# Where q and k are loaded, cast and transposed in an attention and MLP kernel

## The chip, the cores and the metric

The kernel runs on one core of one Trainium2 chip. The metric is the device time of one execution in microseconds. Of nine executions of the kernel before, the median is 354.95 us (353.53 to 356.51). One further execution was recorded by the hardware profiler; every line of a profile in this document is from such an execution. TensorE multiplies matrices, VectorE and ScalarE do elementwise work, GpSimd (POOL) does elementwise work and issues DMA transfers, and SyncE (SP) only issues DMA transfers. In the profile they are PE (PEld for its weight loads), DVE, ACT, POOL and SP; a q after a name means the engine's instruction queue.

## The reference

Eight batches of eight heads, 576 positions, head dimension 64. For each head, with q, k, v in float32 and a vector s:

```python
scores = scale * np.matmul(q, k.transpose(0, 1, 3, 2))
cum = np.cumsum(np.maximum(s, 0.0), axis=-1)
bias = -(cum[:, :, :, None] - cum[:, :, None, :])
scores = np.where(causal, -1e9, scores + np.minimum(bias, 0.0))
attn = softmax(scores)                       # with 1e-9 added to the sum
x = np.matmul(attn, v)                       # -> 4608 tokens x 512
out = (gelu_exact(x @ w_in)) @ w_out         # 512 -> 2048 -> 512
```

The output is 4608 x 512 in float32. The kernel computes the decay as weights on the keys: `wb` holds exp(cum) for each key, v is multiplied by it into `vv`, and the same weights give the denominator.

## The kernel before, in words

The 4608 tokens are taken in nine chunks of 512 (the loop over `c`, L554). Chunk c does three things: layer 1 of its tokens (`l1_item`, 64 matmuls that fill `h_ps`, L472), layer 2 (`l2_item`, 64 matmuls that fill `o_ps`, L491, in four parts of 16 matmuls, each copied by VectorE to one of three `o_sb` buffers at L498 and written out by SP at L500), and, between the parts of layer 2, the attention of batch nb = c + 1. A batch is 576 tokens, so attention stays ahead of the MLP. Attention of a batch goes by pairs of heads (four pairs): scores (`sc_item`, L366, from `qkT`), exp on ScalarE (L372), the causal mask on VectorE (L381, L386), then `av_item` (L394: `avn` the numerator, `avd` the denominator, `avr` for the last 64 positions), and the normalised result goes to `xT`, which layer 1 reads.

The order on every engine is that of the program: the schedule is written by hand, and an engine that waits holds up all that is behind it in its own queue. Waits follow from the program's order: an instruction waits for those ahead of it in the text that write what it reads, or that use what it overwrites.

How q and k reach `qkT` (two of them, used in turn by even and odd batches):

- Batches 0 and 1: `load_early` has POOL issue DMA transfers that cast float32 to bfloat16 on the way, in runs of nine rows of one head (2304 bytes read, 1152 written). TensorE transposes them (`tr_item`, L349) and VectorE copies the result to `qkT` (L354).
- Batches 2 to 7: `load_qk` (L151) has SP issue one float32 load for q and one for k, in runs of six rows (1536 bytes), into one buffer each. POOL casts them in eight pieces (`cast`, L166) into `qk_bf`, with the two heads of a pair beside each other. SP writes `qk_bf` to DRAM (`write_rows`, L174) and reads it back with eight transposing DMA transfers (`transpose_rows`, L181), for four pairs, q and k each.

v of each batch is loaded by SP in five transfers (`load_v`, L192) into one of two buffers, scaled by VectorE (`scale_v`, L220) and reduced to its largest magnitude (`absmax_v`, L210). `absmax` (L203) reduces q and k of a pair from `qkT`. These maxima decide at the very end whether the fast path was safe to use.

In a chunk from 1 to 6 SP's row is: v of batch nb + 1, rows of nb + 1 for q and k, loads of q and k of nb + 2; then the output of part 0, the transposes of pair 0 of batch nb + 1, output 1, the transposes of pair 1, output 2, the transposes of pairs 2 and 3, output 3. VectorE's row is: `scale_v(nb)`, `absmax_v(nb)`, `absmax(c, p)` for the four pairs of batch c, and then the masks, normalisations and `o_sb` copies of the chunk.

Of the kernel before, what the change touches and what calls it, by code (L numbers as in the profile page):

```python
# [19 lines left out]
def kernel(  # L20
# [10 lines left out]
    nc = tc.nc  # L31
    fp32 = mybir.dt.float32
    bf16 = mybir.dt.bfloat16
# [5 lines left out]
    B, H, S, D = q.shape  # L39
    scale = 1.0 / (D ** 0.5)  # L40
    BH = B * H
    ST = 5
    NR = 6
    PR = S // NR
    SL = S - 512
    NP = H // 2
    dff = moe_w_in.shape[1]
    KO = (H * D) // 128
# [46 lines left out]
    G = 9  # L95
    early = {}

    def load_early(b, n, p, both=False):
        src = q if n == "q" else k
        if b == 0 and p == 0:  # L100
            early[n] = work.tile([128, 2, 2, 2, G * D], bf16, tag=f"raw{n}", bufs=1, name=f"early_{n}")
        e0 = (p // 2) * 64
        out = early[n][e0 : e0 + 64, b, p % 2]
        if both:
            out = early[n][e0 : e0 + 64, b].rearrange("g j e f -> g (j e) f")
        ap = [[G * D, 64], [S * D, 4 if both else 2], [1, G * D]]
        nc.gpsimd.dma_start(
            out=out,
            in_=bass.AP(tensor=src.tensor, offset=src.offset + (b * H + 2 * p) * S * D, ap=ap),
        )  # L110
# [21 lines left out]
    w_in_r = const.tile([128, KO, dff], bf16, name="w_in_r")  # L132
    w_out_r = const.tile([128, FT, KO * 128], bf16, name="w_out_r")
    vv = [const.tile([128, ST, H, D], bf16, name=f"vv{i}") for i in range(2)]
    qkT = [const.tile([128, 2, NP, 640], bf16, name=f"qkT{i}") for i in range(2)]
# [8 lines left out]

    def load_qk(b, n, p0, p1, eng):
        src = q if n == "q" else k
        if p0 == 0:
            raws[b, n] = work.tile([PR, H, NR, D], fp32, tag=f"raw{n}", bufs=1, name=f"raw_{n}")  # L150
        eng.dma_start(  # L151
            out=raws[b, n][:, 2 * p0 : 2 * p1].rearrange("p h r d -> p h (r d)"),
            in_=bass.AP(
                tensor=src.tensor,
                offset=src.offset + b * H * S * D + 2 * p0 * S * D,
                ap=[[NR * D, PR], [S * D, 2 * (p1 - p0)], [1, NR * D]],
            ),
        )

    qk_of = {}  # L160

    def cast(b, n, p, eng):
        i = 0 if n == "q" else 1
        if (b, i) not in qk_of:
            qk_of[b, i] = work.tile([PR, NP, NR, 2, D], bf16, tag="qkbf", bufs=2, name="qk_bf")
        eng.tensor_copy(  # L166
            qk_of[b, i][:, p].rearrange("p r e d -> p e r d"), raws[b, n][:, 2 * p : 2 * p + 2]
        )

    rows_of = {}  # L170

    def write_rows(b, i, eng):
        rows_of[b, i] = t = dram.tile([NP, S, 128], bf16, name=f"rows{b}_{i}")
        eng.dma_start(  # L174
            out=t.rearrange("j (p r) c -> p j (r c)", r=NR),
            in_=qk_of.pop((b, i)).rearrange("p j r e d -> p j (r e d)"),
        )

    def transpose_rows(b, p):
        for i in range(2):  # L180
            nc.sync.dma_start_transpose(out=qkT[b % 2][:, i, p, :S], in_=rows_of[b, i][p])  # L181

    def v_tile(b):
        raws[b, "v"] = work.tile([128, ST, H, D], fp32, tag="rawv", bufs=2, name="raw_v")

    def load_v(b, engs):
        if (b, "v") not in raws:
            v_tile(b)
        t = raws[b, "v"]
        for st in range(ST):  # L190
            n_st = 128 if st < ST - 1 else SL
            engs[st % len(engs)].dma_start(  # L192
                out=t[:n_st, st, :, :],
                in_=bass.AP(
                    tensor=v.tensor,
                    offset=v.offset + b * H * S * D + st * 128 * D,
                    ap=[[D, n_st], [S * D, H], [1, D]],
                ),
            )
# [143 lines left out]
    def tr_item(b, p, i):  # L343
        t_ps = ps.tile([128, G, 64], bf16, tag="av", bufs=3, name="tr_ps")
        e0 = (p // 2) * 64
        src = early["qk"[i]]
        for r in range(G):
            for e in range(2):
                nc.tensor.transpose(  # L349
                    t_ps[e * 64 : e * 64 + 64, r, :],  # L350
                    src[e0 : e0 + 64, b, p % 2, e, r * D : (r + 1) * D],
                    ident_bf[e0 : e0 + 64, e0 : e0 + 64],
                )
        nc.vector.tensor_copy(  # L354
            qkT[b % 2][:, i, p, :S].rearrange("d (g r) -> d g r", r=G), t_ps.rearrange("d r g -> d g r")
        )
# [186 lines left out]
    scale_pair(0, 3)  # L543
    for i in range(4):
        load_w(1, i)
    for p in (0, 2):
        for n in "qk":
            load_early(1, n, p, both=True)
    for p in range(NP):
        av_item(0, p, wide=p in (1, 2), rest=False)  # L550
    nc.gpsimd.memset(amv, 0.0)
    nc.gpsimd.memset(ones, 1.0)

    for c in range(NCH):  # L554
        nb = c + 1
        l1_item(c, 0, 0, KO - 1)
        l1_item(c, 1, 0, KO - 1)
        if c == 0:
            for p in range(NP):
                av_rest(0, p)  # L560
            norm_rest(0)
        l1_item(c, 0, KO - 1)
        l1_item(c, 1, KO - 1)
        l1_item(c, 2, av=True)
        if 0 < c and nb < B:
            if nb + 1 < B:
                load_v(nb + 1, [nc.sync])
                for i, n in enumerate("qk"):
                    for p in range(NP):
                        cast(nb + 1, n, p, nc.gpsimd)  # L570
                    write_rows(nb + 1, i, nc.sync)
            if nb + 2 < B:
                for n in "qk":
                    load_qk(nb + 2, n, 0, NP, nc.sync)
            scale_v(nb, STS, nc.vector)
            absmax_v(nb)
        if c == 0:
            absmax_v(0)
        if c < B:
            for p in range(NP):  # L580
                absmax(c, p)
        for f2 in range(3, FT // 2):
            l1_item(c, f2)
        if c == 0:
            exp_set()
            l2_item(c, 0, av=True)
            load_v(1, [nc.sync])
            for n in "qk":
                load_qk(2, n, 0, NP, nc.sync)
            tr_pair(1, 0)  # L590
            tr_pair(1, 1)
            l2_item(c, 1, 0, 4)
            tr_pair(1, 2)
            l2_item(c, 1, 4, 8)
            tr_pair(1, 3)
            sc_item(1, 0)
            l2_item(c, 1, 8)
            load_v(2, [nc.sync])
            for i, n in enumerate("qk"):
                for p in range(NP):  # L600
                    cast(2, n, p, nc.gpsimd)
            sc_item(1, 1)
            l2_item(c, 2, 0, 6, av=True)
            sc_item(1, 2)
            scale_pair(1, 0)
            l2_item(c, 2, 6, 12, av=True)
            sc_item(1, 3)
            scale_pair(1, 1)
            l2_item(c, 2, 12, av=True)
            l2_item(c, 3, 0, 4)  # L610
            for i in range(2):
                write_rows(2, i, nc.sync)
            av_item(1, 0)
            scale_pair(1, 2)
            scale_pair(1, 3)
            l2_item(c, 3, 4, 8)
            av_item(1, 1, wide=True)
            l2_item(c, 3, 8, 12)
            av_item(1, 2, wide=True)
            l2_item(c, 3, 12)  # L620
            av_item(1, 3)
            norm_rest(1)
            for p in range(NP):
                transpose_rows(2, p)
            for n in "qk":
                load_qk(3, n, 0, NP, nc.sync)
            absmax_v(1)
            cert_decay()
        elif nb < B:
            exp_set()  # L630
            l2_item(c, 0, 0, 4)
            sc_item(nb, 0)
            l2_item(c, 0, 4)
            for p in range(1, NP):
                if nb + 1 < B:
                    transpose_rows(nb + 1, p - 1)
                sc_item(nb, p)
                av_item(nb, p - 1)
                l2_item(c, p, 0, 12)
                if p == NP - 1:  # L640
                    if nb + 1 < B:
                        transpose_rows(nb + 1, p)
                    av_item(nb, p)
                    norm_rest(nb)
                l2_item(c, p, 12)
        else:
            if c == B - 1:
                cert_1()
            for sub in range(4):
                l2_item(c, sub, av=sub % 2 == 0)  # L650
                if c == B - 1 and sub < 3:
                    (cert_2, cert_3, cert_4)[sub]()
# [151 lines left out]
```

## Time and profile before

| | |
|---|---|
| median of nine executions | 354.95 us |
| the profiled execution | 354.31 us |
| its span, first to last instruction | 352.5 us |
| PE busy | 321.7 us (91%) |
| ACT busy | 202.1 us (57%) |
| DVE busy | 195.0 us (55%) |
| POOL busy | 60.7 us (17%) |
| DMA moved | 54.38 MB |
| DMA queue of SP (q1) | 86160 packets, 47.35 MB |
| DMA queue of POOL (q0) | 6464 packets, 6.55 MB |
| median time to landing of raw_q / raw_k / rows / a transpose | 12.7 / 14.7 / 5.6 / 3.4 us |

The page gives each engine's busy time, then the span in 40 slices of 8.8 us with the busy share in tenths, the clock that TensorE was granted, and the share of the 16 DMA engines; then the chain of work that ended last, followed back from the end; then groups of instructions by line. In a line of a timeline the first number is the start in microseconds from the span's start, the second the duration. A line of waits reads: who waited, for whom, microseconds in total, how many times, the longest. A landing time is counted from the start of the issue of a transfer to its last byte.

### The profile page before, as it was taken

Reading aid. Unit: us, or ns where it says so; the run is one execution under the profiler, and the core shown is the slowest. Engines: PE = TensorE matmul, PEld = TensorE weight load, DVE = VectorE, ACT = ScalarE, POOL = GpSimd, SP = SyncE. Lnnn points to the kernel's source line nnn. Section 1 sums busy time; section 2 is a strip of 40 time slices with the busy share of each in tenths; the row PEclk is TensorE's granted clock in tenths of the full one; section 3 lists DMA queues with packets and bytes.
Section 4 is the critical chain, followed back from the end, with each engine's and each line's share of the span. In section 5 each row is a group of like instructions: output and inputs, shape, how many; then the busy total and the mean of one; then the engine's idle time right before and its main releaser. Section 6 shows DMA issues by size and latency. Waiting matters only on the chain.

```text
span 352.5 us, 6310 instructions
## 1 busy us (share of the span) xinstructions
PE 321.7 (91%) x2538; PEld 164.7 (47%) x2538; DVE 195.0 (55%) x363; ACT 202.1 (57%) x286; POOL 60.7 (17%) x85
## 2 busy tenths in 40 slices
PE   1778999899999557999999999999999999999993
PEld 1553454544554224544554455445544554444441
DVE  4596576799650295478357745764485548050011
ACT  2676628587666441675777676767576757403500
POOL 6590000700240700340070015000000000000000
PEclk9999999999999986999999999999999999999999
DMA  7999969994999989999999999772430100011011
GB/s 150 157 206 198 191 143 215 227 244 104 236 235 257 210 179 284 234 169 234 267 178 185 270 231 201 150 184 65 130 63 0 56 37 31 0 62 60 0 62 66
DMA packets 92660, 54.38 MB, mean 154 GB/s; under 512 B 67984, under 2 KB 87952, under 8 KB 92624
## 3 DMA queue, kind: packets, MB, share of 16 engines
q1 hardware_dynamic: 86160, 47.35, 60.9%
q0 software_dynamic: 6464, 6.55, 11.2%
q8 instruction: 22, 0.36, 0.4%
q14 instruction: 14, 0.11, 0.1%
HBM read 36.85 MB, written 16.52 MB: 151 GB/s over the span
## 4 chain that ended last, share of the span: by engine, by line
PE 70%; DVE 13%; SPq 5%; DMA 5%; ACT 3%; issue 2%; POOL 0%; DVEq 0%; ACTq 0%; POOLq 0%
PE o_ps L491 31%; PE h_ps L472 27%; PE sc_ps L366 4%; SPq L192 4%; DMA out_dram<-o_sb 4%; DVE vv L220 3%; PE avn L394 3%; DVE amx L203 3%; PE avd L394 2%; DVE amv L210 2%; DMA early_k<-in_k_dram 2%; DVE qkT L354 2%; ACT P L372 1%; SPq L151 1%; PE tr_ps L349 1%
## 5 line engine op out<-in xcount | busy, mean ns | idle before, releaser
L491 PE MATMUL o_ps<-w_out_r,gT 128*128 128x512 bf16 x576 | 136.5, 387 | 4.0 <-DVE o_sb L498 4.0
L472 PE MATMUL h_ps<-xT,w_in_r 128*128 128x512 bf16 x576 | 126.3, 379 | 2.0 <-DVE xT L427 1.4
L372 ACT ACTIVATE P<-sc_ps 128x1024 bf16<-128x1024 f32 x64 | 62.0, 1021 | 49.8 <-PE sc_ps L366 49.8
L472 PEld LDWEIGHTS <-w_in_r 128*128 128x128 bf16 x576 | 56.1, 98 | 69.9 <-issue 2.7
L491 PEld LDWEIGHTS <-gT 128*128 128x128 bf16 x576 | 53.9, 99 | 67.4 <-issue 9.3
L478 ACT ACTIVATE gT<-h_ps 128x1024 bf16<-128x1024 f32 x54 | 54.3, 1022 | 47.2 <-PE h_ps L472 47.1
L498 DVE COPY o_sb<-o_ps 128x512 f32<-128x512 f32 x36 | 24.7, 687 | 74.5 <-PE o_ps L491 58.9
L381 DVE TENSOR_TENSOR P<-P,tri_bf 128x512 bf16<-128x512 bf16 x61 | 27.3, 451 | 40.8 <-ACT P L372 40.2
L166 POOL CAST qk_bf<-raw_q 96x768 bf16<-96x768 f32 x24 | 20.5, 890 | 142.9 <-DMA raw_q<-in_q_dram 142.9
L203 DVE TENSOR_REDUCE amx<-qkT 128x2 f32<-128x1152 bf16 x32 | 40.9, 1335 | 0.0
L427 DVE SCALAR_TENSOR_TENSOR xT<-avn,ln 128x256 bf16<-128x256 f32 (+3 forms) x64 | 21.6, 384 | 23.6 <-ACT ln L412 23.6
L220 DVE TENSOR_TENSOR vv<-raw_v,wb 128x512 bf16<-128x512 f32 (+2 forms) x46 | 29.5, 700 | 0.0
L411 ACT ACTIVATE ln<-avd 128x256 f32<-128x256 f32 x56 | 18.6, 391 | 18.6 <-PE avd L394 18.6
L366 PE MATMUL sc_ps<-qkT 64*128 64x256 bf16 (+2 forms) x320 | 22.4, 266 | 3.7 <-DVE qkT L354 3.6
L394 PEld LDWEIGHTS <-vv 128*64 128x64 bf16 x384 | 18.0, 114 | 15.7 <-issue 12.1
L412 ACT ACTIVATE ln<-ln 128x512 f32<-128x512 f32 (+1 forms) x40 | 23.5, 587 | 1.3
L481 ACT ACTIVATE gT<-h_ps 128x512 bf16<-128x512 f32 x36 | 19.6, 603 | 6.3 <-PE h_ps L472 6.3
L394 PE MATMUL avn<-P,vv 128*64 128x256 bf16 x224 | 16.8, 274 | 6.8 <-DVE P L381 6.1
L210 DVE TENSOR_REDUCE amv<-raw_v 128x1 f32<-128x2048 f32 (+1 forms) x16 | 22.9, 1470 | 0.0
L366 PEld LDWEIGHTS <-qkT 64*128 64x128 bf16 x320 | 13.9, 99 | 18.4 <-issue 11.7
L166 POOL CAST qk_bf<-raw_k 96x768 bf16<-96x768 f32 x24 | 20.3, 885 | 4.1 <-DMA raw_k<-in_k_dram 1.6
L394 PEld LDWEIGHTS <-wb 128*64 128x64 bf16 x384 | 18.2, 116 | 0.2
(79 smaller groups left out, 140.5 us busy)
## 6 DMA issues: line engine op xcount, KB each, us to landing
out_dram<-o_sb SPq DMA_DIRECT2D x36, 256.0 KB, 2.6
raw_v<-in_v_dram SPq DMA_DIRECT2D x32, 256.0 KB, 5.0
raw_q<-in_q_dram SPq DMA_DIRECT2D x6, 1152.0 KB, 12.7
raw_k<-in_k_dram SPq DMA_DIRECT2D x6, 1152.0 KB, 14.7
rows<-qk_bf SPq DMA_DIRECT2D x12, 576.0 KB, 5.6
w_in_r<-in_moe_w_in_dram POOLq DMA_DIRECT2D x4, 512.0 KB, 8.1
w_out_r<-in_moe_w_out_dram POOLq DMA_DIRECT2D x4, 512.0 KB, 13.1
raw_v<-in_v_dram SPq DMA_DIRECT2D x8, 128.0 KB, 4.5
```

What stands on the lines that cost most here:

```text
L166: eng.tensor_copy(qk_of[b, i][:, p].rearrange("p r e d -> p e r d"), raws[b, n][:, 2 * p : 2 * p + 2])
L203: nc.vector.tensor_reduce(amx[:, b * NP + p], qkT[b % 2][:, :, p, :S], axis=AX, op=ALU.max, apply_absolute_value=True)
L210: nc.vector.tensor_reduce(amv[:n_st, b, j : j + 1], t[:n_st, st0:st1].rearrange("p s h d -> p (s h d)"), axis=AX, op=ALU.max, apply_absolu ...
L220: eng.tensor_tensor(vb[:n_st, st0:st1, h0:h1, :], t[:n_st, st0:st1, h0:h1, :], wb[:n_st, st0:st1, b * H + h0 : b * H + h1] .unsqueeze(3).t ...
L366: nc.tensor.matmul(s_ps[:, e, off : off + n], lhsT=qkT[b % 2][e * 64 : e * 64 + 64, 1, p, jt * 128 : jt * 128 + 128], rhs=qkT[b % 2][e * 6 ...
L372: nc.scalar.activation(P[:, :, UO[u] : UO[u] + UW[u]], s_ps[:, :, : UW[u]], func=AF.Exp, scale=scale)
L381: eng.tensor_tensor(d, d, tri_bf.unsqueeze(1).unsqueeze(1).to_broadcast([128, 2, 2, 128]), op=MULT)
L394: nc.tensor.matmul(out[e * 64 : e * 64 + 64, lo : lo + n], lhsT=(wb[:, jt, b * H + h : b * H + h + 1].to_broadcast([128, 64]) if den else ...
L472: nc.tensor.matmul(h_of[c, f2][i], lhsT=w_in_r[:, ko, ft * 128 : (ft + 1) * 128], rhs=xT[:, ko, c * NB % XW : c * NB % XW + NB], start=(ko ...
L478: nc.scalar.activation(gT_of[c][:, f2 * 2 : f2 * 2 + 2, :], hh_of[c, f2], func=AF.Gelu)
L491: nc.tensor.matmul(o_ps, lhsT=gT[:, ft, sub * 128 : (sub + 1) * 128], rhs=w_out_r[:, ft, :], start=(ft == 0), stop=(ft == FT - 1),)
L498: nc.vector.tensor_copy(o_sb, o_ps)
```

## The change

`load_qk` is rewritten: for batches 1 to 7 it calls `load_early` four times (two pairs at a time, q and k), so that all q and k come by POOL's casting transfers in runs of 2304 bytes, into one of three buffers for q and one of three for k. POOL's eight casts become four copies (`interleave`) from bfloat16 to bfloat16 that set the two heads of a pair beside each other, and the rows are written in runs of 2304 bytes. v of batch 1 is issued earlier: POOL first writes a few elements of its buffer from the last columns of `w_in_r`, so that SP's loads wait until w_in is there. Batches 2 and 3 are loaded by POOL before the loop begins; in chunk c POOL copies batch nb + 1 and then issues the loads of nb + 2. In chunks 1 to 5 the eight transposes of batch nb + 1 are issued right behind its rows, at the head of the chunk, ahead of `absmax` and of the chunk's outputs; in chunk 0, pairs 0 and 1 of batch 2 stand before output 3 and pairs 2 and 3 behind it.

```diff
     def load_early(b, n, p, both=False):
-        if b == 0 and p == 0:
-            early[n] = work.tile([128, 2, 2, 2, G * D], bf16, tag=f"raw{n}", bufs=1, name=f"early_{n}")
+        if p == 0:
+            early[b, n] = work.tile([128, 2, 2, G * D], bf16, tag=f"raw{n}", bufs=3, name=f"early_{n}")
...
-    def load_qk(b, n, p0, p1, eng):
-            raws[b, n] = work.tile([PR, H, NR, D], fp32, tag=f"raw{n}", bufs=1, name=f"raw_{n}")
-        eng.dma_start(
...
-    def cast(b, n, p, eng):
-            qk_of[b, i] = work.tile([PR, NP, NR, 2, D], bf16, tag="qkbf", bufs=2, name="qk_bf")
-        eng.tensor_copy(
-            qk_of[b, i][:, p].rearrange("p r e d -> p e r d"), raws[b, n][:, 2 * p : 2 * p + 2]
-        )
...
+    def load_qk(b):
+        for p in (0, 2):
+            for n in "qk":
+                load_early(b, n, p, both=True)
+    def interleave(b, n):
+        t = qk_of[b, i] = work.tile([128, 2, G, 2, D], bf16, tag="qkbf", bufs=2, name="qk_bf")
+        for j in range(2):
+            nc.gpsimd.tensor_copy(
+                t[:, j].rearrange("g r e d -> g e r d"),
+                early[b, n][:, j].rearrange("g e (r d) -> g e r d", r=G),
+            )
...
+    load_qk(1)
+    v_tile(1)
+    nc.gpsimd.tensor_copy(
+        raws[1, "v"][:, :, 0, 0], w_in_r[:, KO - 1, dff - 1 : dff].to_broadcast([128, ST])
+    )
+    load_v(1, [nc.sync])
...
+    for b in (2, 3):
+        load_qk(b)
+    for n in "qk":
+        interleave(2, n)
...
                 load_v(nb + 1, [nc.sync])
                 for i, n in enumerate("qk"):
-                    for p in range(NP):
-                        cast(nb + 1, n, p, nc.gpsimd)
+                    interleave(nb + 1, n)
                     write_rows(nb + 1, i, nc.sync)
-            if nb + 2 < B:
-                for n in "qk":
-                    load_qk(nb + 2, n, 0, NP, nc.sync)
+                if nb + 2 < B:
+                    load_qk(nb + 2)
+                for p in range(NP):
+                    transpose_rows(nb + 1, p)
             scale_v(nb, STS, nc.vector)
             absmax_v(nb)
...
             for p in range(1, NP):
-                if nb + 1 < B:
-                    transpose_rows(nb + 1, p - 1)
                 sc_item(nb, p)
```

More of the change, by code (lines that the diff above doesn't have):

```diff
@@ L42 @@
     ST = 5
-    NR = 6
-    PR = S // NR
     SL = S - 512
@@ L99, in load_early @@
         src = q if n == "q" else k
-        if b == 0 and p == 0:
-            early[n] = work.tile([128, 2, 2, 2, G * D], bf16, tag=f"raw{n}", bufs=1, name=f"early_{n}")
+        if p == 0:
+            early[b, n] = work.tile([128, 2, 2, G * D], bf16, tag=f"raw{n}", bufs=3, name=f"early_{n}")
         e0 = (p // 2) * 64
-        out = early[n][e0 : e0 + 64, b, p % 2]
+        out = early[b, n][e0 : e0 + 64, p % 2]
         if both:
-            out = early[n][e0 : e0 + 64, b].rearrange("g j e f -> g (j e) f")
+            out = early[b, n][e0 : e0 + 64].rearrange("g j e f -> g (j e) f")
         ap = [[G * D, 64], [S * D, 4 if both else 2], [1, G * D]]
@@ L143 @@
     raws = {}
-    def load_qk(b, n, p0, p1, eng):
-        src = q if n == "q" else k
-        if p0 == 0:
-            raws[b, n] = work.tile([PR, H, NR, D], fp32, tag=f"raw{n}", bufs=1, name=f"raw_{n}")
[L151 to L157, printed above, removed]
-        )
+    def load_qk(b):
+        for p in (0, 2):
+            for n in "qk":
+                load_early(b, n, p, both=True)
     qk_of = {}
-    def cast(b, n, p, eng):
+    def interleave(b, n):
         i = 0 if n == "q" else 1
-        if (b, i) not in qk_of:
-            qk_of[b, i] = work.tile([PR, NP, NR, 2, D], bf16, tag="qkbf", bufs=2, name="qk_bf")
-        eng.tensor_copy(
-            qk_of[b, i][:, p].rearrange("p r e d -> p e r d"), raws[b, n][:, 2 * p : 2 * p + 2]
-        )
+        t = qk_of[b, i] = work.tile([128, 2, G, 2, D], bf16, tag="qkbf", bufs=2, name="qk_bf")
[4 more added lines that the diff above has]
+            )
     rows_of = {}
     def write_rows(b, i, eng):
-        rows_of[b, i] = t = dram.tile([NP, S, 128], bf16, name=f"rows{b}_{i}")
+        rows_of[b, i] = t = dram.tile([2, 2, S, 128], bf16, name=f"rows{b}_{i}")
         eng.dma_start(
-            out=t.rearrange("j (p r) c -> p j (r c)", r=NR),
+            out=t.rearrange("j a (g r) c -> (a g) j (r c)", r=G),
             in_=qk_of.pop((b, i)).rearrange("p j r e d -> p j (r e d)"),
@@ L180, in transpose_rows @@
         for i in range(2):
-            nc.sync.dma_start_transpose(out=qkT[b % 2][:, i, p, :S], in_=rows_of[b, i][p])
+            nc.sync.dma_start_transpose(out=qkT[b % 2][:, i, p, :S], in_=rows_of[b, i][p % 2, p // 2])
     def v_tile(b):
@@ L345, in tr_item @@
         e0 = (p // 2) * 64
-        src = early["qk"[i]]
+        src = early[b, "qk"[i]]
         for r in range(G):
@@ L350, in tr_item @@
                     t_ps[e * 64 : e * 64 + 64, r, :],
-                    src[e0 : e0 + 64, b, p % 2, e, r * D : (r + 1) * D],
+                    src[e0 : e0 + 64, p % 2, e, r * D : (r + 1) * D],
                     ident_bf[e0 : e0 + 64, e0 : e0 + 64],
@@ L545 @@
         load_w(1, i)
-    for p in (0, 2):
-        for n in "qk":
-            load_early(1, n, p, both=True)
+    load_qk(1)
[4 more added lines that the diff above has]
+    load_v(1, [nc.sync])
     for p in range(NP):
@@ L568 @@
                 for i, n in enumerate("qk"):
-                    for p in range(NP):
-                        cast(nb + 1, n, p, nc.gpsimd)
+                    interleave(nb + 1, n)
                     write_rows(nb + 1, i, nc.sync)
-            if nb + 2 < B:
-                for n in "qk":
-                    load_qk(nb + 2, n, 0, NP, nc.sync)
+                if nb + 2 < B:
+                    load_qk(nb + 2)
+                for p in range(NP):
+                    transpose_rows(nb + 1, p)
             scale_v(nb, STS, nc.vector)
@@ L586 @@
             l2_item(c, 0, av=True)
-            load_v(1, [nc.sync])
-            for n in "qk":
-                load_qk(2, n, 0, NP, nc.sync)
             tr_pair(1, 0)
@@ L598 @@
             load_v(2, [nc.sync])
-            for i, n in enumerate("qk"):
-                for p in range(NP):
-                    cast(2, n, p, nc.gpsimd)
+            for i in range(2):
+                write_rows(2, i, nc.sync)
             sc_item(1, 1)
@@ L610 @@
             l2_item(c, 3, 0, 4)
-            for i in range(2):
-                write_rows(2, i, nc.sync)
+            for p in (0, 1):
+                transpose_rows(2, p)
             av_item(1, 0)
@@ L622 @@
             norm_rest(1)
-            for p in range(NP):
+            for p in (2, 3):
                 transpose_rows(2, p)
-            for n in "qk":
-                load_qk(3, n, 0, NP, nc.sync)
             absmax_v(1)
@@ L640 @@
                 if p == NP - 1:
-                    if nb + 1 < B:
-                        transpose_rows(nb + 1, p)
                     av_item(nb, p)
```

## The prediction

> **What bounds the kernel now.** I read the page's slices first, then the windows by chunk, then the chain of work that ended last, then the waits, and at the end the timelines of SP and DVE in one quiet chunk.
>
> ```profile
> span 352.5 us, 6310 instructions
> PE   1778999899999557999999999999999999999993
> PEclk9999999999999986999999999999999999999999
> DMA  7999969994999989999999999772430100011011
> ```
>
> TensorE is full except at the start, at the end and in slices 13 to 15 (115 to 141 us), where the granted clock drops too. The windows, cut at the first layer-1 matmul of each chunk, give the size of that hole (start:end, length, PE busy, then the other engines):
>
> ```profile
> 69.03:103.66 34.63, 34.63 (x271) 17.74 (x266) 27.55 (x55) 25.37 (x38) 6.81 (x9) 1.00 0.89 199
> 103.66:152.98 49.32, 39.23 (x266) 19.54 (x265) 22.50 (x37) 24.20 (x35) 13.37 (x16) 0.90 1.08 238
> 222.09:256.65 34.56, 34.56 (x266) 17.65 (x264) 20.77 (x37) 23.94 (x35) 0.00 (x0) 1.00 0.57 134
> ```
>
> A chunk with attention in it takes 34.56 us and is pure TensorE time. Chunk 2 takes 49.32, so 14.8 us are lost there, and nowhere else after chunk 0. The chain and the waits say why:
>
> ```profile
> 104.86 2.82 SPq L151
> 107.78 13.02 DMA out_dram<-o_sb
> 121.52 3.56 DVE vv L220 x4
> 128.75 5.04 DVE amx L203 x4
> 134.17 0.96 PE avn L394 x8
> DVE o_sb L498 <- DMA out_dram<-o_sb: 15.7, 1, 15.7
> PE avn L394 <- DVE P L381: 6.1, 1, 6.1
> ```
>
> SP still issues v, q and k loads when the outputs of chunk 1 are ready. The first output is issued at 107.8 and lands 13.0 us later behind 2.3 MB of q and k; the three `o_sb` buffers are full; VectorE waits 15.7 us at L498, and its scales, reduces and masks are late for TensorE. What TensorE feels is set by VectorE's order: after the last `amx` reduce (128.75 + 5.04 = 133.8) come masks and then `avn` at 134.2.
>
> One chunk with no q or k load in it, and one uninterrupted row of eight transposes:
>
> ```profile
> 224.17 0.34 SPq L500 DMA_DIRECT2D out_dram<-o_sb  x1
> 224.56 4.58 SPq L192 DMA_DIRECT2D raw_v<-in_v_dram  x5
> 229.24 1.09 SPq L174 DMA_DIRECT2D rows<-qk_bf  x2
> 229.86 5.11 DVE L203 TENSOR_REDUCE amx<-qkT 128x2 f32<-128x1152 bf16 x4
> 75.24 11.11 SPq L181 DMA_TRANSPOSE qkT<-rows  x8
> ```
>
> **What the skill says.** The Trainium skill, DMA: Bandwidth & Descriptors, Anatomy of one DMA, says that a semaphore wait of a DMA is taken on the issuing sequencer, before dispatch; the trace agrees: everything on SP stands behind one waiting transfer (5.05 and 5.56 us for one v load in the chain). The same page, SWDGE vs HWDGE vs iDMA, says that a cast during the DMA can be issued from GpSimd only, so the new loads leave SP's queue for good; w_in and the early q and k of before are of this kind. The same page, Queues, rings and completion order, says that the DMA engines take turns between queues packet by packet, so the moved loads still share the engines with v, rows and transposes; no view of before has a cast load beside a transpose. TensorE: Matmul & The Clock Gate, Part 1, gives half clock after an idle window of about 3.4 us, and the trace agrees: after idle times of 4.0 and 6.1 us the stretch 133.78 to 152.98 had a granted clock of 0.84.
>
> **The change, part by part.** *q and k loads.* Twelve SP loads of 1152 KB (L151) go. From issue plus landing, raw_q landed at 94.6 and raw_k at 99.4: 4.8 us of transfer for one tensor. Instead POOL issues 24 casting loads of 288 KB; the early ones landed 1.4 us apart (43.2, 44.6), so 2.8 us per tensor and 5.7 for q and k. Issuing costs POOL 4 x 0.63 = 2.5 us a batch. This frees about 4 us of transfer a batch and all of SP's L151 time (2.8 + 1.4 us ahead of the late output). It removes the hole of chunk 2: -14.8.
>
> *Casts.* Eight POOL casts of 96x768 (0.89 us) become four copies of 128x1152; by elements 0.89 x 1152 / 768 = 1.3 us, 5.3 a batch. POOL is 17% busy and is now a batch ahead, so they cost nothing; without that cover rows would be 5.3 late.
>
> *Rows* keep their bytes, in longer runs (2304 B instead of 1536): 0 to -1 us, I take 0.
>
> *v of batch 1* moves from 47 us to about 29.6 (w_in landed at 28.7), beside w_out and the early loads of batch 1. v takes about 6 us of transfers (at its 47 to 55 us rate less the issue time), so the early loads land up to 6 us later than their 40.4 to 44.6 us, against transposes that start at 46. Between -2 (TensorE idles 2.7 us in chunk 0, some behind late work) and +4; I take +1.
>
> *Transposes of batch nb+1.* These move most. Before, each pair stood between the outputs of chunk c, after `absmax(c, p)` in program order. Now all eight stand at the head of chunk c, ahead of it. They write `qkT[(nb+1) % 2]`, which is `qkT[c % 2]`, and that is what `absmax(c, p)` reads. So each reduce of chunks 1 to 5 now reads what the transposes of the same chunk write and has to wait for their landing (the built program has a wait for both landings on each of the 20 reduces; the maxima noted for batches 1 to 5 become those of 3 to 7). VectorE is in order: behind it wait the masks, then `avn` on TensorE, the `o_sb` copies, and so the outputs. This new chain, from the start L of layer 1:
>
> - L to v issue on SP: 224.56 - 222.09 = 2.5
> - v issue to k rows landed: rows issued at 229.2 and 229.9 land 5.1 and 6.3 us later, so 236.2 - 224.56 = 11.7
> - k rows landed (77.3 in the eight-transpose row) to the last landing (last issue 85.1 + 2.7 = 87.8): 10.5
> - the last reduce: 1.3
> - end of reduces to the next L: in chunk 2 of before 152.98 - 133.78 = 19.2, clock loss included (at full clock it would be 222.09 - 206.10 + 0.4 = 16.4)
>
> Sum 45.2, against 34.56: +10.6 a chunk. TensorE reaches `avn` at L + 18.6 (on its timeline 206.10 in the chunk that starts at 187.53) and the reduces end at L + 26, so it stands still some 7.5 us each time.
>
> Chunk 1 is worse: SP starts its v load only after out 3 of chunk 0 (about 70) and the last four transposes of batch 2 (4 x 1.3, with waits), so near L + 7 instead of L + 2.5: +4.5. Batches 5, 6 and 7 are loaded by POOL once rows of chunks 1, 2 and 3 have landed, that is just beside the transposes: between 0 and +5.7 each, I take 1. Batch 4 falls beside v and rows of chunk 1: 0 to +5.7, I take 1.
>
> **Sum** against the span: chunk 0 +1; chunk 1 10.6 + 4.5 + 2 = 17.1; chunks 2 and 3, 11.6 each, 23.2; chunks 4 and 5, 21.2; hole of chunk 2 -14.8. Together +47.7: span 400.2. The profiled execution took 354.31, 1.8 more than its span: 402.0; the median of the runs is 0.6 above that execution: 402.6.
>
> **Rivals.**
> *A shorter chain.* Rows land 3 us sooner in an emptier queue, and the clock recovers at once: 45.2 - 3 - 2.8 = 39.4, +4.8 a chunk. 5 x 4.8 + 5.5 - 14.8 = +14.7: 369.6 as its end, up to 388. For it: the DMA share falls. Against: the chunk priced above had no q or k load either, and the clock did drop.
> *POOL's loads win the engines.* All four contended batches cost 5.7 instead of 1: +18.8, 421. For it: long packets taking turns with 256 B ones. Against: eight transposes are paced by SP's 1.3 us issue and leave gaps.
> *Not slower: the reduce wait is hidden.* If the last transposes land by L + 16.9 (18.6 less 0.4 and the reduce), VectorE is in time, the hole of chunk 2 is gone and the time is 354.95 - 14.8 + 1 = 341. The chain to the last landing has to shrink from 24.7 to 16.9, and SP's issue times alone (2.5 + 4.6 + 1.1 + 8 x 1.26 = 18.3) are past that; only an earlier start of SP's row could do it, so hardly.
> *No effect* would need both to cancel: no mechanism does that.
>
> **How the numbers follow.** Forecast 66% (its own range 390 to 415), shorter chain 15%, POOL's loads 14%, hidden wait 4%, no difference 1%. About 0.3% is what a measurement of this kernel can tell from no change. The range 378 to 420 takes in the upper half of the shorter chain and most of the contention case. Faster 0.04, same 0.01, slower 0.95.
>
> **What would show it.** Right: `amx` waits for qkT landings in five chunks, some 10 us or more each; `avn` waits for the mask in the same five; the clock dips five times; chunks 1 to 5 of about 52, 46, 46, 45, 45 us, from chunk 6 on as before; no wait of `o_sb` on out_dram. Wrong: chunks of 34.6 us with the reduces done before the masks are wanted, or transposes that land within 17 us of layer 1.

## The result, and the profile after

The changed kernel takes 415.81 us, the median of ten executions (411.91 to 418.29), where the kernel before took 354.75 beside it (352.92 to 356.51). The ratio is 1.1709, with a 95% interval from 1.1678 to 1.174. The profiled execution took 414.44 us, its span is 412.7.

The slices of the page, for the kernel after:

```profile
span 412.7 us, 6315 instructions
PE   2789986992089980999439993999399999999994
PEclk9999995997569995899959998899889999999999
DMA  8999999998901879109961383119311001002011
```

A slice is 10.3 us here, and a hole is a stretch in which TensorE has little to do. Before, there was one after chunk 0; now there are five (slices 10 and 11, 16, 20 and 21, 25, 29). The granted clock is near half in slice 7 and in the first three of them. The DMA engines are busy in the first three holes and nearly idle behind each of the five (slices 12 and 13, 17 and 18, 22, 26 and 27, 30). While TensorE stands still, transfers are under way, and behind each hole few are left.

The windows of the kernel after, cut at the first layer-1 matmul of each chunk (start:end, length, busy time of PE, PEld, DVE, ACT and POOL, then clock, DMA share, GB/s), for chunks 0 to 6:

```profile
26.76:76.35 49.59, 42.78 (x441) 21.92 (x441) 29.41 (x48) 24.70 (x36) 15.82 (x22) 0.90 1.12 213
76.35:134.02 57.67, 37.32 (x270) 19.05 (x265) 25.59 (x55) 25.47 (x38) 9.13 (x12) 0.79 0.74 134
134.02:182.37 48.35, 36.75 (x266) 18.93 (x264) 20.69 (x37) 24.05 (x35) 6.82 (x8) 0.86 0.58 121
182.37:230.73 48.36, 36.19 (x266) 18.75 (x265) 20.68 (x36) 24.05 (x35) 6.82 (x8) 0.89 0.60 120
230.73:274.12 43.39, 37.15 (x265) 19.02 (x264) 20.97 (x39) 24.05 (x35) 4.42 (x4) 0.92 0.41 107
274.12:316.35 42.23, 35.92 (x266) 18.72 (x265) 20.78 (x37) 24.05 (x35) 0.00 (x0) 0.92 0.42 110
316.35:350.90 34.55, 34.55 (x265) 17.64 (x264) 20.77 (x36) 23.94 (x35) 0.00 (x0) 1.00 0.09 31
```

Chunks 1 to 5 are all long; chunk 6, the first without transposes, has the 34.55 us of before. Layer 1 of chunk 1 begins 7.3 us later than before (76.35 against 69.03). The rest of the difference is +23.0 in chunk 1, -1.0 in chunk 2 (whose old hole is gone), +13.8, +8.8, +7.7 in chunks 3 to 5, and 0.5 behind them: 60.2 in all, which is 412.7 - 352.5.

The waits of the kernel after (who, for whom, total us, times, longest):

```profile
DVE amx L194 <- DMA qkT<-rows: 77.0, 17, 11.6
PE avn L385 <- DVE P L372: 56.7, 5, 20.4
```

VectorE waits for the landings of the transposes before its reductions, 77 us in sum, and TensorE waits five times for the causal mask that stands behind these reductions. VectorE's old wait of 15.7 us for an `o_sb` buffer is not in the list any more. In the chain of waits (start, us, what), the ends of chunks 2 and 4 look like this:

```profile
152.48 8.85 DMA qkT<-rows
161.42 0.98 DVE amx L194
162.97 0.98 issue
164.42 0.96 PE avn L385 x8
...
251.31 2.63 DMA qkT<-rows
...
254.03 0.17 DVE amx L194
...
255.76 0.96 PE avn L385 x8
...
274.28 13.81 PE h_ps L463 x64
```

In both, `avn` follows on a reduction, and that on a transpose. In chunk 4 the transpose is on the chain for 2.6 us, in chunk 2 for 8.9: what stretches it is the subject of the second experiment.

### The profile page after: what moved, and what is told of

Its sections match the earlier page's. It is cut to its first block, busy times and chain, and to the rows that moved or that the text cites. A ratio compares the mean times of both kernels' runs of the same rounds, so it can differ in the third digit from the quotient of the medians.

```text
span 412.7 us, 6315 instructions
## 1 busy us (share of the span) xinstructions
PE 331.8 (80%) x2538; PEld 170.9 (41%) x2538; DVE 192.2 (47%) x363; ACT 202.6 (49%) x286; POOL 61.1 (15%) x86
## 4 chain that ended last, share of the span: by engine, by line
PE 63%; DMA 20%; SPq 11%; DVE 3%; issue 2%; POOL 1%; DVEq 0%
PE o_ps L482 27%; PE h_ps L463 25%; DMA qkT<-rows 8%; DMA raw_v<-in_v_dram 7%; SPq L183 6%; SPq L172 5%; PE avn L385 4%; DMA w_in_r<-in_moe_w_in_dram 3%; PE avd L385 3%; PE sc_ps L357 2%; DVE amx L194 2%; DMA rows<-qk_bf 1%; PE avr L385 1%; PE avw L385 1%; DVE P L372 1%
## 5 line engine op out<-in xcount | busy, mean ns | idle before, releaser
L482 PE MATMUL o_ps<-w_out_r,gT 128*128 128x512 bf16 x576 | 140.7, 396 | 0.0
L482 PEld LDWEIGHTS <-gT 128*128 128x128 bf16 x576 | 54.8, 101 | 65.8 <-issue 9.0
L194 DVE TENSOR_REDUCE amx<-qkT 128x2 f32<-128x1152 bf16 x32 | 42.1, 1346 | 77.0 <-DMA qkT<-rows 77.0
L385 PE MATMUL avn<-P,vv 128*64 128x256 bf16 x224 | 18.7, 296 | 60.4 <-DVE P L372 56.7
L385 PEld LDWEIGHTS <-vv 128*64 128x64 bf16 x384 | 20.8, 124 | 70.7 <-issue 63.8
L156 POOL COPY qk_bf<-early_q 128x1152 bf16<-128x1152 bf16 x12 | 13.6, 1168 | 160.0 <-DMA rows<-qk_bf 155.2
L211 DVE TENSOR_TENSOR vv<-raw_v,wb 128x512 bf16<-128x512 f32 (+2 forms) x46 | 26.6, 636 | 3.6 <-issue 2.3
L357 PEld LDWEIGHTS <-qkT 64*128 64x128 bf16 x320 | 14.0, 98 | 18.0 <-issue 12.7
L385 PEld LDWEIGHTS <-wb 128*64 128x64 bf16 x384 | 21.0, 128 | 0.5
L385 PE MATMUL avd<-P,wb 128*64 128x256 bf16 x224 | 18.5, 293 | 0.0
## 6 DMA issues: line engine op xcount, KB each, us to landing
early_k<-in_k_dram POOLq DMA_DIRECT2D x14, 288.0 KB, 10.2
w_in_r<-in_moe_w_in_dram POOLq DMA_DIRECT2D x4, 512.0 KB, 10.3
```

What stands on the lines that cost most here:

```text
L194: nc.vector.tensor_reduce(amx[:, b * NP + p], qkT[b % 2][:, :, p, :S], axis=AX, op=ALU.max, apply_absolute_value=True)
L211: eng.tensor_tensor(vb[:n_st, st0:st1, h0:h1, :], t[:n_st, st0:st1, h0:h1, :], wb[:n_st, st0:st1, b * H + h0 : b * H + h1] .unsqueeze(3).t ...
L357: nc.tensor.matmul(s_ps[:, e, off : off + n], lhsT=qkT[b % 2][e * 64 : e * 64 + 64, 1, p, jt * 128 : jt * 128 + 128], rhs=qkT[b % 2][e * 6 ...
L385: nc.tensor.matmul(out[e * 64 : e * 64 + 64, lo : lo + n], lhsT=(wb[:, jt, b * H + h : b * H + h + 1].to_broadcast([128, 64]) if den else ...
L482: nc.tensor.matmul(o_ps, lhsT=gT[:, ft, sub * 128 : (sub + 1) * 128], rhs=w_out_r[:, ft, :], start=(ft == 0), stop=(ft == FT - 1),)
```

## The experiments

Times are medians, ratios stand against the kernel before run beside them. In the changed kernel, and in the second, third, fourth and seventh experiment, the maxima of q and k noted for batches 1 to 5 are taken from what the transposes have just written, so from batches 3 to 7, and those of batches 1 and 2 are not taken at all; in the others each is that of its own batch.

### 1. The transposes behind the reductions

```diff
-                for p in range(NP):
-                    transpose_rows(nb + 1, p)
             scale_v(nb, STS, nc.vector)
...
             for p in range(NP):
                 absmax(c, p)
+        if 0 < c and nb + 1 < B:
+            for p in range(NP):
+                transpose_rows(nb + 1, p)
```

SP issues the same eight transposes in the same order; only their place against `absmax` in the text of the program differs.

> The changed kernel, with the eight transposes of a chunk still at its head on SP but behind absmax in program order, so that a reduce no longer reads what they write (they wait for the reduce instead, which is done 13 us into the chunk). If the wait of the reduces is what costs, chunks 1 to 5 fall from 57.7, 48.4, 48.4, 43.4 and 42.2 us to about 34.6 each and the time to 348 us. If it is the traffic of POOL's loads beside transposes and rows, the time stays above 390.

Measured: 348.82 us (346.36 to 349.67), ratio 0.9786 [0.972, 0.9852]. So 67 of the 415.8 us hang on this order alone. The group of the reductions in the page of this kernel (last, the idle time ahead of it):

```profile
L194 DVE TENSOR_REDUCE amx<-qkT 128x2 f32<-128x1152 bf16 x32 | 40.9, 1335 | 0.0
```

And from its waits:

```profile
DVE o_sb L489 <- DMA out_dram<-o_sb: 6.5, 1, 6.5
```

The reductions wait for nothing now. Chunk 2 still lasts 39.5 us (layer 1 begins at 108.16 and 147.70): the outputs of chunk 1 stand on SP behind eight transposes until 108.7, and VectorE waits for the buffer.

### 2. The loads of the next batch behind the transposes

```diff
-                if nb + 2 < B:
-                    load_qk(nb + 2)
                 for p in range(NP):
                     transpose_rows(nb + 1, p)
+                if nb + 2 < B:
+                    nc.gpsimd.tensor_copy(pace, qkT[(nb + 1) % 2][:, 1, NP - 1, S - 1 : S])
+                    load_qk(nb + 2)
```

The small copy makes POOL wait for the last transpose. The reductions still read behind the transposes.

> The changed kernel, with POOL's loads of batch nb + 2 held until the last transpose of batch nb + 1 has landed (one copied element), so that no casting load runs beside transposes; the reduces still wait. If the loads hold the transposes up, chunks 2 and 3 fall from 48.4 to the 43 us of chunks 4 and 5, and chunk 1 from 57.7 to about 47: 395 us. If they share the engines without harm, 413 to 418.

Measured: 394.54 us (392.12 to 397.34), ratio 1.1121 [1.1039, 1.1203]. Starts of layer 1 at 74.31, 122.36, 166.34, 208.64 and 251.85 give chunks of 48.1, 44.0, 42.3 and 43.2 us where the changed kernel has 57.7, 48.4, 48.4 and 43.4. The gain lies in chunks 1 to 3, where the changed kernel has a load beside the transposes, and there is none in chunk 4, where it has not.

The landings of the eight transposes of one chunk (us from issue to landing, least, median and longest): chunk 2 of the changed kernel first, then chunk 2 of this one.

```profile
DMA to landing us min/median/max: 2.4/6.0/8.8
```

```profile
DMA to landing us min/median/max: 2.5/2.6/2.7
```

The median issue on SP took 1.24 us in both, and the row of eight 11.35 against 10.41 us. Beside casting loads a transpose of this chunk takes up to 8.8 us to land. The prediction had cited the Trainium skill (DMA: Bandwidth & Descriptors, Queues, rings and completion order) for queues that take turns packet by packet; this agrees in so far as the loads of one queue delay the transposes of another, but the turns themselves are not seen in these views. Slow landings are not peculiar to casting loads: in the kernel before, a transpose issued at 109.0 beside SP's own float32 loads landed 12.3 us later.

### 3. The kernel before, with the transposes ahead of the reductions

```diff
                     write_rows(nb + 1, i, nc.sync)
+            if nb + 1 < B:
+                for p in range(NP):
+                    transpose_rows(nb + 1, p)
             if nb + 2 < B:
...
-                if nb + 1 < B:
-                    transpose_rows(nb + 1, p - 1)
```

Nothing else of the change is in it: SP's float32 loads and POOL's casts are those of before.

> The kernel before with one edit: the eight transposes of a chunk right behind its rows, ahead of absmax (and of the q and k loads on SP). All loads and casts are the old ones. If the place of the transposes alone makes the slowdown, chunks 1 to 5 take 43 to 46 us: 385 to 400 us. If the new loads are needed for it, 355.

Measured: 413.22 us (410.14 to 415.71), ratio 1.1624 [1.1526, 1.1721]. The order alone makes the old kernel as slow as the changed one. Its waits:

```profile
DVE amx L203 <- DMA qkT<-rows: 81.9, 20, 29.8
PE avn L394 <- DVE P L381: 61.9, 5, 33.5
```

Chunks 2 to 4 last 44.0 to 44.1 us and chunk 5 44.6, so 9.5 to 10 us over 34.56, near the 10.6 of the prediction, with no load beside the transposes (SP issues it behind them). I had expected 385 to 400; the excess is chunk 1, 70 us long. There SP issues v of batch 3 only at 87.5, behind eight transposes of batch 2 and the loads of batch 3 (86.3 and 86.9); raw_k lands at 99.5, the casts end at 102.7, the rows land at 107.9, and `avn` starts at 120.1. The number was missed, the mechanism not.

### 4. v of batch 1 loaded where it was

```diff
-    v_tile(1)
-    nc.gpsimd.tensor_copy(
-        raws[1, "v"][:, :, 0, 0], w_in_r[:, KO - 1, dff - 1 : dff].to_broadcast([128, ST])
-    )
-    load_v(1, [nc.sync])
...
             l2_item(c, 0, av=True)
+            load_v(1, [nc.sync])
```

> The changed kernel, with v of batch 1 issued where the kernel before issues it (behind the first output). If its early place costs the 7 us of chunk 0, 409 us. If POOL's loads of batches 2 and 3, queued to 64 us, are what it competes with, v lands near 65 us all the same: 413 to 418.

Measured: 415.79 us (414.3 to 416.79), ratio 1.1701 [1.1634, 1.1769]: the total is that of the changed kernel. Layer 1 of chunk 1 begins at 73.91 instead of 76.35, but experiments with the chunk 0 of the changed kernel have it at 72.95 to 74.93. The early place of this load isn't what lengthens chunk 0, and it gains nothing either: v issued at 47.3 lands at 58.6 to 62.1, v issued from 30.9 on lands as late as 64.9, for the loads of batches 1, 2 and 3 and of `w_out` share the engines with it.

### 5. Both repairs: reductions first, loads last

The edits of experiments 1 and 2 together: behind the reductions come the transposes, and behind these the small copy and the load of batch nb + 2.

> Both repairs at once: transposes behind the reduces in program order, and POOL's loads of batch nb + 2 held until the transposes of batch nb + 1 have landed. In the first experiment one hole was left in chunk 2 (40.0 instead of 34.6 us): VectorE waited 6.5 us for an o_sb buffer, since the outputs of chunk 1 stood on SP behind transposes that the loads had slowed. If that is so, chunk 2 falls to 34.6: 343.5 us. If the hole has another cause, 348 to 350.

Measured: 344.69 us (344.22 to 345.62), ratio 0.9734 [0.9692, 0.9777]. This beats the kernel before. Chunks 1 to 5 last 34.6 us each (chunk 2 had 39.5 in experiment 1, not the 40.0 of the expectation), the `o_sb` wait is gone, for SP's transposes of chunk 1 are done at 102.1 instead of 108.6. What is left is chunk 0: layer 1 of chunk 1 begins at 72.95 where it was 69.03.

### 6. The load of batch 2 behind v of batch 1

The kernel of experiment 5, with two edits ahead of the loop:

```diff
-    for b in (2, 3):
-        load_qk(b)
+    nc.gpsimd.tensor_copy(pace[:SL], raws[1, "v"][:SL, ST - 1, 0, 0:1])
+    load_qk(2)
     for n in "qk":
         interleave(2, n)
+    load_qk(3)
```

> As the experiment before, and in chunk 0 POOL's loads of batch 2 wait until v of batch 1 has landed (one copied element), those of batch 3 stand behind the copies of batch 2. If those loads are what held v of batch 1 up to 62 to 65 us, v lands near 52 us, chunk 0 falls from about 48 to 43 us and the time to 338.5 us. If not, 343 to 345.

Measured: 345.72 us (345.12 to 345.92), ratio 0.9756 [0.9716, 0.9797]. v landed at 50.8, as expected, and chunk 1 begins at 73.30 all the same. So late v was only one of two limits. VectorE's timeline in this kernel shows the other; POOL's copies of batch 2 ran from 59.56 to 64.76:

```profile
58.10 0.43 DVE L372 TENSOR_TENSOR P<-P,tri_bf 128x512 bf16<-128x512 bf16 x1 [0.49 <-ACT P L363]
58.45 0.22 DVE L377 TENSOR_TENSOR P<-P,tri_bf 128x128 bf16<-128x128 bf16 x1
58.58 0.88 DVE L211 TENSOR_TENSOR vv<-raw_v,wb 128x512 bf16<-128x512 f32 x2
...
61.03 1.16 DVE L377 TENSOR_TENSOR P<-P,tri_bf 128x128 bf16<-128x128 bf16 x1
62.11 2.78 DVE L211 TENSOR_TENSOR vv<-raw_v,wb 128x512 bf16<-128x512 f32 x2
```

The same instructions take 0.22 and 0.44 us before POOL starts and 1.16 and 1.39 beside it, about the length of one POOL copy in this stretch (1.28, half of the 2.55 us of two).

### 7. The reductions at the end of the chunk

The changed kernel, with `absmax` of chunks 1 to 5 moved behind all other work of VectorE in its chunk, so that it still reads what the transposes of the chunk wrote:

```diff
-        if c < B:
+        if c in (0, 6, 7):
             for p in range(NP):
                 absmax(c, p)
...
+        if 0 < c < 6:
+            for p in range(NP):
+                absmax(c, p)
     fast.close()
```

> The changed kernel, with the reduces of chunks 1 to 5 moved to the end of the chunk on VectorE and nothing else: they still read what the transposes of batch nb + 1 write (so the maxima kept for batches 1 to 5 are those of 3 to 7, as in the changed kernel) and still depend on their landing, but no mask, copy or normalisation stands behind them by then. If the place in VectorE's row is what turns the wait into lost time, 347 to 351 us. If the dependency costs wherever it stands, above 390.

Measured: 347.59 us (346.53 to 348.2), ratio 0.9813 [0.977, 0.9857]. The transposes are as early as in the change, and read by the same reductions; only the masks don't stand behind them any more. What costs the time is thus the queue on VectorE and hardly the transposes' place on SP: that leaves 1.4 us in chunk 2 (36.0 long), where VectorE waits 4.6 us for an `o_sb` buffer.

### 8. POOL's copies behind the scaling of v

The kernel of experiment 6; in chunk 0 the copies of batch 2, its rows, the load of batch 3 and the first transposes come behind VectorE's last scaling of v of batch 1:

```diff
...
             scale_pair(1, 3)
+            nc.gpsimd.tensor_copy(pace, vv[1][:, 0, H - 1, 0:1])
+            for i, n in enumerate("qk"):
+                interleave(2, n)
+                write_rows(2, i, nc.sync)
+            load_qk(3)
+            for p in (0, 1):
+                transpose_rows(2, p)
...
```

> The kernel with batch 2 loaded behind v of batch 1, and the reductions first and loads last, took 345.72, and its chunk 0 is about 4 us longer than before's although v of batch 1 lands at 50.8. Here POOL's copies of batch 2 wait until VectorE has scaled the last heads of v of batch 1, and rows 2, the loads of batch 3 and the first transposes of batch 2 follow them. Theory: POOL's copies at 59.6 to 64.7 slowed VectorE's masks and v scales beside them (0.44 to about 1.3 us each, some 4.5 us in sum), and TensorE waited 4.3 us for them. Then the masks take 0.43 and the scales 0.44 again, the wait of 4.3 us is gone, and the time is about 341.5. Rival: the same instructions take as long without copies beside them (it is the DMA traffic, or chunk 0 is held by another wait): 345 to 346, with the slow instructions still there.

Measured: 343.81 us (342.14 to 345.08), ratio 0.9685 [0.9623, 0.9746]. VectorE in this kernel, at the same place as above:

```profile
60.71 0.21 DVE L377 TENSOR_TENSOR P<-P,tri_bf 128x128 bf16<-128x128 bf16 x1
60.84 0.88 DVE L211 TENSOR_TENSOR vv<-raw_v,wb 128x512 bf16<-128x512 f32 x2
```

Back to 0.21 and 0.44 us each. Layer 1 of chunk 1 begins at 68.56, 4.7 us sooner than in experiment 6 and 0.5 sooner than in the kernel before. DMA traffic isn't the reason for the slow instructions, then: from 60.7 to 64.7 us the DMA engines moved 238 GB/s in experiment 6 and 247 here. It is POOL's copies. But the gain was mostly given back: the transposes of batches 2 and 3 are later by what the copies were delayed, SP has the outputs of chunk 1 behind them until 109.7, VectorE waits 6.8 us for an `o_sb` buffer, and chunk 2 lasts 39.5 us.

### 9 and 10. The transposes between the outputs

Number 9 is the kernel of experiment 8, number 10 the changed kernel itself, each with the transposes of chunks 1 to 5 in the places of the kernel before (number 9 with the load of nb + 2 behind the last pair):

```diff
             for p in range(1, NP):
+                if nb + 1 < B:
+                    transpose_rows(nb + 1, p - 1)
                 sc_item(nb, p)
...
                 if p == NP - 1:
+                    if nb + 1 < B:
+                        transpose_rows(nb + 1, p)
```

> The kernel with the copies of batch 2 behind the v scaling, with one more edit: in chunks 1 to 5 the transposes of batch nb + 1 stand between the outputs, pair by pair, where the kernel before had them, and the loads of nb + 2 behind the last pair. In its parent chunk 1 begins at 68.6 (73.0 without the late copies), but chunk 2 lasts 39.5 instead of 34.6, because the outputs of chunk 1 stand on SP behind eight transposes until 109.7 and VectorE waits 6.8 us for an o_sb buffer. Theory: with an output ahead of each pair of transposes that wait is gone and the 4.4 us gained in chunk 0 stay: chunks 1 to 5 of 34.6, time about 339. Rival: batch 2 is late on its whole way (loads, rows, transposes), and the lateness shows elsewhere, at the scores of batch 3 in chunk 2 or in the landings of the last pairs: 342 to 345.

> The changed kernel with the transposes of chunks 1 to 5 back in the places of the kernel before, between the outputs, and nothing else changed (loads by POOL, copies, v of batch 1 and chunk 0 as in the change). Theory (their place ahead of the reductions makes all of the slowdown after chunk 0, and an output behind eight transposes made the hole of 5 us in the variant with the transposes behind the reductions): chunk 0 about 47 us, chunks 1 to 5 of 34.6 us, time 344 to 346. Rival (the casting loads beside the transposes delay batch 3 so that TensorE waits for its scores in chunk 2): 348 to 352. If the place of the transposes isn't the cause: over 390.

Measured for number 10: 345.72 us (344.28 to 347.03), ratio 0.9741 [0.9666, 0.9816], as the theory had it. Layer 1 begins at 74.93, 109.50, 144.05 and 178.61, so all chunks after chunk 0 last 34.6 us, although the casting loads still run beside transposes: where nothing urgent stands behind the landing, a slow landing (up to 9.1 us in chunk 1) costs nothing. The rest of the change is a gain of 2.6% (1.8 to 3.3); the place of the transposes turned it into a loss.

Measured for number 9: 341.16 us (340.31 to 342.58), ratio 0.9609 [0.9541, 0.9676], the fastest kernel of the study. Chunk 0 keeps its gain (68.42), chunk 1 lasts 34.6, but chunks 2 and 3 last 36.3 and 35.8, 3.0 us too long together, where a time of 339 had been expected. The reason shows in VectorE's timeline in chunk 2, with POOL's copies of batch 4 from 121.36 on:

```profile
120.45 0.43 DVE L372 TENSOR_TENSOR P<-P,tri_bf 128x512 bf16<-128x512 bf16 x1 [4.43 <-ACT P L363]
121.37 1.41 DVE L372 TENSOR_TENSOR P<-P,tri_bf 128x512 bf16<-128x512 bf16 x1 [0.49 <-ACT P L363]
122.70 1.16 DVE L377 TENSOR_TENSOR P<-P,tri_bf 128x128 bf16<-128x128 bf16 x1
```

This is the cost of experiment 6 again, in another place: the later loads bring POOL's copies to the moment of the first masks. A version that keeps them clear of the masks was not run, and that this would give back the whole 3 us is an inference from these lines.

## Why the prediction was right, and where its sizes were off

**The mechanism held.** The prediction named one chain, from the v issue over rows, transposes and reductions to the mask and `avn`, in five chunks. The waits show it (five waits of `avn` for the mask), experiments 1, 7 and 10 end it in three ways and land at 346 to 349, and experiment 3 makes it in the old kernel. Five clock dips came, chunk 6 was as before, and the `o_sb` wait went. Of the rivals, the hidden wait is out: the last transposes land 23 us or more after the start of layer 1, not 17. Of the shorter chain, half of its 3 us on the rows came (below), and its recovery of the clock did not: chunks 4 and 5 have 0.92.

**One reading of the trace was wrong, though no term of the sum rests on it.** The prediction took the 5.05 and 5.56 us of two v loads in the kernel before for waits on a semaphore. In the list of SP's own waits in that kernel, all v loads together have this:

```profile
SPq L192 <- DVE P L386: 0.4, 1, 0.4
```

The two loads took that long to issue while q and k, 2.3 MB issued just ahead of them, were under way. Waits on SP do occur in that trace, but at the outputs: 125.0 us in all for VectorE's `o_sb` copies.

**In an undisturbed chunk the sum was nearly right.** Chunk 4 has no load beside its transposes. SP's timeline of the kernel after:

```profile
233.34 4.25 SPq L183 DMA_DIRECT2D raw_v<-in_v_dram  x5
237.69 1.08 SPq L165 DMA_DIRECT2D rows<-qk_bf  x2
242.25 10.32 SPq L172 DMA_TRANSPOSE qkT<-rows  x8
```

L to v issue 2.6 (predicted 2.5); v issue to k rows landed at 243.58, 10.2 (11.7); to the last landing at 253.93, 10.4 (10.5); the last reduce and the rest up to layer 1 at 274.1, 20.2 (1.3 + 19.2). Sum 43.4 against 45.2: the rows land 1.5 us sooner. The prediction had taken 0 for their longer runs, and had put rows that land sooner in an emptier queue into a rival. The record speaks for the runs: in the chunk of before that was priced, v was beside the rows as here, and yet the k rows took 6.3 us from issue to landing where they take 5.2 here; with the old runs they take 5.4 to 6.2 in chunks 2 to 5 of experiment 3, with the new ones 5.0 to 5.3 in those of experiments 5 and 10. No experiment changes the runs alone. Chunks 4 and 5 together came out 4.7 us short of the 21.2.

**The 1 us taken for loads beside the transposes, out of a range from 0 to 5.7, was mis-sized.** In chunks 2 and 3 it measured 4.4 and 6.1 us (experiment 2 against the changed kernel), and in the changed kernel's chunks 2 and 3 the excess is 13.8 instead of 11.6, with the quicker rows already in it. The argument for 1 was that SP's issue of one transpose in 1.3 us leaves gaps; the median issue stayed at that pace, but the landing went from 2.6 to as much as 8.8. Here the rival of POOL's loads winning the engines came true within the forecast. In all, experiment 2 gains 22.4 us of span, 2.0 of them in chunk 0, which it doesn't touch; I had 4 for these loads.

**Chunk 1, with 4.5 for SP and 1 + 1 for loads, was to lose 17.1, and it lost 23.0.** From L at 76.35: v issue at 85.70 (+9.35; I had 7), rows landed at 98.43 (+12.7; 11.7), last landing at 113.5 (+15.1; 10.5), the last reduction and gaps to 115.12 (+1.6; 1.3), layer 1 at 134.02 (+18.9; 19.2). The load of batch 4, which I had put beside v and rows, was issued at 76.2 and slowed the last four transposes of batch 2 that SP still had ahead of v: SP needed 8.0 us for them, and 5.9 in experiment 2, where no load runs there.

**The +1 taken for chunk 0, out of a range from -2 to +4, was wrong: it was +7.3.** The prediction asked what v's early place does to the early loads, and not what the loads of batches 2 and 3, which the change puts ahead of the loop, do to v. In the changed kernel the chain to layer 1 of chunk 1 goes through the last landing of v:

```profile
47.13 17.81 DMA raw_v<-in_v_dram
64.96 0.04 DVE vv L211
```

With these loads held back in experiment 6, v is there at 50.8. In the changed kernel and in experiments 1, 2, 4, 5, 7 and 10, the last of v lands at 62.1 to 64.9, and layer 1 of chunk 1 follows 10.6 to 11.8 us later each time, at 72.95 to 76.35; so 7.3 is the upper end of a spread that begins at 3.9.

Behind this limit stood a second. In experiment 6, with v early, POOL's copies of batch 2 run beside VectorE's last masks and scales, and chunk 0 is no shorter; in experiment 8 they come later, and it is as short as before. In the changed kernel itself these copies are done five microseconds before v lands:

```profile
57.48 2.43 POOL L156 COPY qk_bf<-early_k 128x1152 bf16<-128x1152 bf16 x2
```

So late v sets the length of its chunk 0. What the copies would cost in this place with an early v was not run. The second limit shows that one more step of the prediction doesn't hold: "POOL is 17% busy and is now a batch ahead, so they cost nothing": POOL was idle enough, but its neighbour isn't free while it copies. The kernel before has this already, in small. Its masks of 128x512 take 0.42 us with POOL idle, and 0.70 and 0.74 beside POOL's casts:

```profile
212.16 0.70 DVE L381 TENSOR_TENSOR P<-P,tri_bf 128x512 bf16<-128x512 bf16 x1 [0.69 <-ACT P L372]
210.22 3.33 POOL L166 CAST qk_bf<-raw_q 96x768 bf16<-96x768 f32 x4 [24.65 <-DMA raw_q<-in_q_dram]
```

On this the Trainium skill, SBUF — State Buffer, Who interferes with whom, has what the prediction left out: a VectorE instruction with two inputs in SBUF and a GpSimd instruction that reads SBUF shut each other out for the length of an instruction. The lines of experiments 6, 8 and 9 agree: 0.22 us becomes 1.16, with copies of 1.2 to 1.35 us beside it.

Altogether against the predicted span of 400.2: +6.3 in chunk 0, +5.9 in chunk 1, +2.2 each in chunks 2 and 3, -4.7 in chunks 4 and 5, 0.5 behind: 412.6, where 412.7 was measured. The measured time of 415.81 lies just above the forecast's own range of 390 to 415, and within 378 to 420 only because that allowed for most of the contention. That the total is no further off is in part luck: the 4.7 us that chunks 4 and 5 fell short make up for some of the loads and of chunk 0, which were priced too low.

## What to carry to other kernels

When a transfer is moved up in the program, ask first which reader of its buffer now comes behind it instead of ahead: an in-order engine then stops at that reader, with all that is queued after it, and the best loads and casts don't make up for it. Price a transfer beside others by its landing, not by its issue rate, and only where something urgent stands behind that landing. An idle engine isn't free work either: look at what its neighbour does in the same microseconds.

## What the runs showed of the hardware

- Beside casting loads issued by POOL, transposes of SP's queue keep their median issue time (1.24 us) but land in up to 8.8 us instead of 2.6 (chunk 2 of the changed kernel and of experiment 2). v in five transfers, issued from 30.9 on, is not there before 64.9 in the changed kernel; with the loads of batches 2 and 3 held back it is there at 50.8 (experiment 6).
- VectorE's `tensor_tensor` on two SBUF inputs takes 1.16 to 1.41 us instead of 0.22 to 0.44 beside POOL copies from bfloat16 to bfloat16 (experiments 6, 8 and 9).
- A POOL copy of 128x1152 from bfloat16 to bfloat16 with its heads interleaved takes 1.12 us in most places of the changed kernel, shorter than the 1.3 that the prediction estimated by elements from a cast of float32.
